# Attention and a gated feed-forward on one core: other blocks for the transposes of two attention units, and other places and engines for splitting the weights

## The chip, the cores and the metric

The kernel runs on one core of a Trainium2 chip. The metric is the time of one execution on the device in microseconds; the median of a few runs counts. TensorE (PE) multiplies, VectorE (DVE), ScalarE (ACT) and GpSimd (POOL) work on tiles in SBUF, SyncE (SP) starts the transfers. TensorE's results lie in PSUM, in banks that ScalarE or VectorE must empty before TensorE may write there again.

## The reference

Attention with a window (half of the heads plain, half dilated) over 8 batches, 8 heads, 576 positions, 64 dimensions; then a gated feed-forward with an RMS norm over all 4608 tokens.

```python
scores = scale * np.matmul(q, k.transpose(0, 1, 3, 2))
mask_plain = (rel >= 0) & (rel < window)                        # window 32
mask_dil = (rel >= 0) & (rel < window * dilation) & (rel % dilation == 0)
...
attn = np.exp(scores - np.max(scores, axis=-1, keepdims=True))
attn = attn / (np.sum(attn, axis=-1, keepdims=True) + 1e-09)
x = np.matmul(attn, v)            # to (4608, 512)
...
xn = x / np.sqrt(np.mean(x * x, axis=-1, keepdims=True) + 1e-06) * rms_g
g = xn @ w_gate                   # (512, 1536)
silu = g * (1.0 / (1.0 + np.exp(-g)))
return (silu * (xn @ w_val) @ w_out).astype(np.float32)
```

The weights arrive as 64-bit floats, and the kernel itself makes 32-bit ones of them.

## The kernel before

The tokens are cut into 16 units of 288 (`u`). A unit's attention comes in 14 bursts `(u, c, i)`: a pair of heads `c` and a block of queries `i`. A burst has three steps on TensorE, each in a place of its own: scores (`q`), transposing the probabilities (`t`), product with the values (`o`). Each unit's feed-forward has 12 turns `j`, each of three blocks (`part`): gate (`gate`, part 0), value (`val`, part 1), and the projection of the turn before (`proj`, part 2). Unit 1's attention is computed between the blocks of unit 0's feed-forward, unit 2's between those of unit 1's, and so on.

The order of instructions is written by the program itself: `now` counts the blocks, `later(dt, rank, fn)` puts work off by `dt` blocks, and `flush` issues what is due ahead of the block, by rank. `plan` writes into `events` in which block each burst's `q`, `t` and `o` stand. On every engine the instructions then run in this order, each as soon as its semaphores allow. `t` in the code below counts the blocks from the first gate of unit 0 (block 0 to 35 are unit 0's feed-forward, 36 to 71 unit 1's).

Up to unit 1 attention and feed-forward of unit 0 are computed in plain 32-bit floats. From then on each operand is split in a high part (`hi`, a cast) and the rest (`lo`, a subtraction), and three products are summed (`three`, lines 628 to 630). So the names that matter here are:

- `split_weight`: the cast of a weight into `hi` on ScalarE (L243) and, one block later, the subtraction into `lo` (L244), on VectorE or POOL. A weight pair shares one tile `lo`, which takes the place of the 32-bit pair before it. 36 weights are split, in the order of use, from block `SPLITS[0]` on; each must be there before unit 1 needs it (block 36 for the first).
- `decode`: VectorE makes a 32-bit pair out of the raw words in two instructions (L178 and L182), one in each block of unit 0; ScalarE (L160) and POOL (L163) prepare it.
- `split`: the high and low parts of a head's keys (L331 cast, L336 subtraction) and queries (L340, L345); its last step also starts the load of the head after next.
- `untranspose`: ScalarE copies a burst's transposes out of PSUM (L448); from unit 2 on VectorE subtracts that copy from them (L450).
- `bank`: gates and values share two banks. The bank of a value block `v` is that of the next turn's gate; the bank of a gate is that of the next turn's value. Transposes of part 0 and part 1 stand in spare columns of that block's bank, those of part 2 in the bank of the gate just used. Accesses of different engines to one bank are kept in order.
- `tanh` and `silu` (L667, L672) empty the gate's bank, `prod` (L685) the value's; `parts` makes `hhi` (L696) and `hlo` (L697) of it. `take` (L410) empties the bank `o`, `scores_max` (L362, L367) the bank `s`, `scores_norm` ends a burst's normalisation (L386, L387 and then L390 on ScalarE for unit 1 or L393 on POOL).

## Time and profile before

| | |
|---|---|
| median of 3 runs | 1143.98 us (1143.95 to 1144.72) |
| the profiled execution | 1143.79 us, span 1142.0 us |
| granted TensorE clock, mean | 0.997 |
| PE busy | 1119.9 us (98%) |
| DVE, ACT, POOL busy | 786.6 (69%), 714.2 (63%), 613.8 us (54%) |
| DMA | 82.19 MB, mean 72 GB/s |

The page has the busy time of each engine, the span in 40 slices, the chain of work that ended last and the costliest groups of instructions. Besides it the trace can be asked for the busy time in any stretch, for who waited for whom, for groups of instructions in a stretch, and for single instructions in order of time. An idle time in brackets stands with what ended it. Unit 0's feed-forward runs from about 40 to 127 us, unit 1's from 127.3 us on.

### The profile page before, as it was taken

Reading aid. Unit: us, or ns where it says so; the run is one execution under the profiler, and the core shown is the slowest. Engines: PE = TensorE matmul, PEld = TensorE weight load, DVE = VectorE, ACT = ScalarE, POOL = GpSimd, SP = SyncE. Lnnn points to the kernel's source line nnn. Section 1 sums busy time; section 2 is a strip of 40 time slices with the busy share of each in tenths; the row PEclk is TensorE's granted clock in tenths of the full one; section 3 lists DMA queues with packets and bytes.
Section 4 is the critical chain, followed back from the end, with each engine's and each line's share of the span. In section 5 each row is a group of like instructions: output and inputs, shape, how many; then the busy total and the mean of one; then the engine's idle time right before and its main releaser. Section 6 shows DMA issues by size and latency. Waiting matters only on the chain.

```text
span 1142.0 us, 25943 instructions
## 1 busy us (share of the span) xinstructions
PE 1119.9 (98%) x8371; PEld 1088.9 (95%) x8371; DVE 786.6 (69%) x2859; ACT 714.2 (63%) x2622; POOL 613.8 (54%) x1073
## 2 busy tenths in 40 slices
PE   8998989999999999999999999999999999999998
PEld 7776789999999999999999999999999999999998
DVE  7878874868768586776758677675867758586411
ACT  6795676756757576675757666575765757576311
POOL 8234576655656465565646555464655646465211
PEclk9999999999999999999999999999999999999999
DMA  9655210312212131221213112121211312120000
GB/s 253 184 208 204 77 51 26 104 41 71 64 36 84 38 95 43 75 67 31 81 40 97 46 50 84 38 82 41 75 60 47 95 33 79 42 79 15 5 19 21
DMA packets 61545, 82.19 MB, mean 72 GB/s; under 512 B 7298, under 2 KB 41090, under 8 KB 61410
## 3 DMA queue, kind: packets, MB, share of 16 engines
q1 hardware_dynamic: 61410, 80.54, 23.8%
q8 instruction: 67, 1.10, 0.4%
q14 instruction: 68, 0.56, 0.2%
HBM read 71.08 MB, written 9.44 MB: 71 GB/s over the span
## 4 chain that ended last, share of the span: by engine, by line
PE 86%; DVE 5%; ACT 4%; issue 2%; POOL 2%; POOLq 0%; DVEq 0%; ACTq 0%
PE v L628 9%; PE acc L628 8%; PE g L628 8%; PE acc L629 8%; PE v L629 8%; PE g L630 8%; PE v L630 8%; PE g L629 8%; PE acc L630 8%; PE s L495 3%; PE o L483 3%; PE o L484 1%; PE busy L745 1%; ACT t L377 1%; DVE raw L178 1%
## 5 line engine op out<-in xcount | busy, mean ns | idle before, releaser
L697 POOL TENSOR_TENSOR hlo<-th,hhi 128x288 fp32r<-128x288 f32 x180 | 145.4, 808 | 206.2 <-ACT hhi L696 153.8
L630 PE MATMUL acc<-hhi,lo 128*128 128x288 f32 x720 | 212.3, 295 | 0.0
L393 POOL TENSOR_SCALAR t<-t,sum 72x72 f32<-72x72 f32 (+3 forms) x414 | 153.4, 382 | 67.8 <-DVE sum L387 60.3
L630 PE MATMUL v<-xhi,lo 128*128 128x288 f32 x612 | 180.8, 295 | 0.0
L630 PE MATMUL g<-xhi,lo 128*128 128x288 f32 x612 | 180.6, 295 | 0.0
L377 ACT ACTIVATE t<-t,sum 96x128 f32<-96x128 f32 (+3 forms) x448 | 166.1, 375 | 9.7 <-DVE sum L367 9.1
L696 ACT CAST hhi<-th 128x288 fp32r<-128x288 f32 x180 | 78.1, 434 | 142.0 <-DVE th L685 140.2
L306 POOL TENSOR_TENSOR vlo<-vt,vhi 128x128 fp32r<-128x128 f32 x196 | 93.6, 478 | 107.2 <-ACT vhi L302 92.4
L667 ACT ACTIVATE th<-g 128x288 f32<-128x288 f32 x180 | 73.7, 410 | 106.8 <-PE g L630 85.5
L630 PEld LDWEIGHTS acc<-hhi,lo 128*128 128x128 f32 x720 | 135.6, 188 | 0.0
L423 DVE TENSOR_TENSOR xraw<-o,xraw 64x72 f32<-64x72 f32 (+1 forms) x364 | 99.2, 273 | 50.6 <-ACT xraw L413 44.5
L672 DVE SCALAR_TENSOR_TENSOR th<-th,g 128x288 f32<-128x288 f32 x180 | 80.3, 446 | 70.3 <-ACT th L667 70.3
L630 PEld LDWEIGHTS v<-xhi,lo 128*128 128x128 f32 x612 | 115.4, 189 | 0.0
L630 PEld LDWEIGHTS g<-xhi,lo 128*128 128x128 f32 x612 | 115.0, 188 | 0.0
L628 PE MATMUL g<-xhi,hi_g 128*128 128x288 f32 x357 | 110.7, 310 | 1.9 <-DVE pt L450 1.5
L628 PE MATMUL acc<-hhi,hi_o 128*128 128x288 f32 x360 | 110.9, 308 | 0.0
L336 POOL TENSOR_TENSOR ks<-qk,ks 128x288 fp32r<-128x288 f32 (+2 forms) x112 | 108.8, 986 | 0.0
L685 DVE TENSOR_TENSOR th<-th,v 128x288 f32<-128x288 f32 x180 | 81.5, 453 | 39.6 <-PE v L630 31.2
L629 PE MATMUL acc<-hlo,hi_o 128*128 128x288 f32 x360 | 107.0, 297 | 0.0
L362 DVE TENSOR_TENSOR t<-s,mask 96x256 f32<-96x256 f32 (+3 forms) x196 | 71.5, 365 | 49.7 <-PE s L495 44.4
L413 ACT COPY xraw<-o 64x72 f32<-64x72 f32 (+1 forms) x364 | 93.9, 258 | 11.8 <-PE o L484 9.7
L629 PE MATMUL g<-xlo,hi_g 128*128 128x288 f32 x322 | 94.8, 295 | 0.0
(189 smaller groups left out, 3588.9 us busy)
## 6 DMA issues: line engine op xcount, KB each, us to landing
qk<-in_qk_dram SPq DMA_DIRECT2D x60, 288.0 KB, 2.8
vt<-in_v_dram SPq DMA_DIRECT2D x196, 64.0 KB, 1.9
qk<-in_qk_dram SPq DMA_DIRECT2D x30, 352.0 KB, 3.0
out_dram<-ot SPq DMA_DIRECT2D x64, 144.0 KB, 1.9
qk<-in_qk_dram SPq DMA_DIRECT2D x30, 304.0 KB, 2.8
raw<-in_w_gate_dram SPq DMA_DIRECT2D x12, 512.0 KB, 4.8
raw<-in_w_val_dram SPq DMA_DIRECT2D x12, 512.0 KB, 4.5
raw<-in_w_out_dram SPq DMA_DIRECT2D x12, 512.0 KB, 4.2
```

What stands on the lines that cost most here:

```text
L306: G.tensor_tensor(out=vl, in0=vs.pop(b), in1=vh, op=ALU.subtract)
L336: ek.tensor_tensor(out=ks[:, 1, :nkt], in0=kr, in1=ks[:, 0, :nkt], op=ALU.subtract)
L377: A.activation(out=t[:nq, a, :n], in_=t[:nq, a, :n], func=AF.Exp, scale=-1.0, bias=sm[:nq, a, 0:1], accum_out=sm[:nq, a, 1:2] if u or i % ...
L393: (V if u == 0 and (c, i) > (NC - 1, 0) else G).tensor_scalar(out=t[:nq, a, :n], in0=t[:nq, a, :n], scalar1=sm[:nq, a, 3:4], scalar2=1.0, ...
L413: A.copy(out=to[a * D:(a + 1) * D], in_=o[a * D:(a + 1) * D, (2 + a) * nq:(3 + a) * nq])
L423: V.tensor_tensor(out=to[rows], in0=o[rows, a * nq:(a + 1) * nq], in1=to[rows], op=ALU.add)
L628: PE.matmul(out, wh[:, cc, :], xh, start=start, stop=False)
L629: PE.matmul(out, wh[:, cc, :], xl, start=False, stop=False)
L630: PE.matmul(out, wl[:, cc, :], xh, start=False, stop=stop)
L672: V.scalar_tensor_tensor(out=t, in0=t, scalar=1.0, in1=g, op0=ALU.add, op1=ALU.mult)
L685: V.tensor_tensor(out=t, in0=t, in1=v_ps[:, :U], op=ALU.mult)
L697: G.tensor_tensor(out=lo, in0=t, in1=hi, op=ALU.subtract)
```

## The change

Five edits. First, the table of blocks for unit 1's bursts and a new one like it for unit 2's: `q` in parts 0 and 1, so `t` (five blocks on) in parts 2 and 0, where before unit 1's stood mostly in 0 and 1, and unit 2's, spread evenly over more blocks, in all three. Unit 2's first scores stand in block 33 in place of 30. When a unit's sum and norm stand is unchanged. Second, splitting of weights in unit 0: in blocks of part 2 from 5 to 30, nine of them, where before it was every even block from 4 to 30, fourteen. Third, from block 35 on (before: 37) one weight in each block: in odd blocks VectorE now does the cast as well as the subtraction, in even blocks ScalarE the cast and POOL the subtraction, as before. Fourth, unit 2's first two heads are split six blocks later, with the keys' subtraction on VectorE instead of POOL. Fifth, all sums of unit 1's squares are on VectorE (two of three were on POOL).

```diff
-SPLITS = 4, 31, 37
+SPLITS = 5, 31, 35
-EARLY, LAST = (-6, -9), 17
+SCORES = {1: (-3, -2, 0, 1, 3, 4, 6, 7, 9, 10, 12, 13, 15, 16),
+          2: (-3, -2, 0, 1, 3, 4, 6, 7, 9, 10, 12, 13, 15, 16)}
+EARLY, LAST = -9, 17
...
-    def split_weight(kind, j, e):
+    def split_weight(kind, j, e, alone):
...
-        A.copy(out=hi, in_=single(kind, j))
+        (e.tensor_copy if alone and e is V else A.copy)(out=hi, in_=single(kind, j))
         later(1, 5.5, lambda: e.tensor_tensor(out=lo, in0=single(kind, j), in1=hi, op=ALU.subtract))
...
-            later(1, 0.4, lambda: (V if c == NC - 1 else G).tensor_tensor(out=xsq[u], in0=xsq[u], in1=sq, op=ALU.add))
+            later(1, 0.4, lambda: (V if c == NC - 1 or u == 1 else G).tensor_tensor(out=xsq[u], in0=xsq[u], in1=sq, op=ALU.add))
...
-                        later(5 + a, 9, lambda a=a: split(NNAT, a, (1, 2, 2, 3), G, V))
+                        later(11 + a, 9, lambda a=a: split(NNAT, a, (1, 2, 2, 3), V, V))
...
-        events.setdefault(base + o_at[-1] + (4 if u == 1 else 3), {})["sum"] = u
-        events.setdefault(base + o_at[-1] + (4, 7, 5)[min(u, 2)], {})["apply"] = u
+        last = base + (o_at[-1] if u < NNAT else LAST + 8)
+        events.setdefault(last + (4 if u == 1 else 3), {})["sum"] = u
+        events.setdefault(last + (4, 7, 5)[min(u, 2)], {})["apply"] = u
...
-        q_at = [LAST - (LAST - EARLY[u > NNAT]) * (nb - 1 - k) // (nb - 1) for k in range(nb)]
+        q_at = [LAST - (LAST - EARLY) * (nb - 1 - k) // (nb - 1) for k in range(nb)]
         t_at, o_at = [t + 5 for t in q_at], [t + 8 for t in q_at]
-        if u < NNAT:
-            q_at = (-4, -2, -1, 1, 2, 4, 6, 7, 8, 10, 11, 13, 14, 16)
-            t_at, o_at = [t + 5 for t in q_at], [t + 7 for t in q_at]
+        if u <= NNAT:
+            q_at = SCORES[u]
+            t_at, o_at = [t + 5 for t in q_at], [t + (7 if u < NNAT else 8) for t in q_at]
...
-                if used and (t >= SPLITS[2] or t % 2 == 0 and SPLITS[0] <= t < SPLITS[1]):
-                    later(0, 6, lambda: split_weight(*used.pop(0), V if t < SPLITS[1] or t % 2 else G))
+                if used and (t >= SPLITS[2] or part == 2 and SPLITS[0] <= t < SPLITS[1]):
+                    later(0, 6, lambda: split_weight(*used.pop(0), V if t < SPLITS[1] or t % 2 else G, t >= SPLITS[2]))
```

What it moves, at three places. In the rows the name before the arrow is what is written; names carry unit, turn or burst and a running number, `x2` is twice in a row. The changed kernel's line numbers are higher by four. First, TensorE in unit 0, from the end of the value block of turn 1 to the gate block of turn 2; before:

```order
L625 MATMUL v_0_1_696<-xn_3_623,f_1_332 128x288
L465 MATMUL v_0_1_696<-ident_64,t_1_0_2_598 128x96 x2
L492 MATMUL s_1_1_2_701<-qk_1_1_118 96x128 x2
L625 MATMUL acc_0_0_718<-h_0_640,f_2_529 128x288
L625 MATMUL acc_0_1_720<-h_0_640,f_2_529 128x288
L625 MATMUL acc_0_2_722<-h_0_640,f_2_529 128x288
L625 MATMUL acc_0_3_724<-h_0_640,f_2_529 128x288
L474 MATMUL o_1_0_1_726<-pt_1_0_1_678,v_1_0_150 128x192
L625 MATMUL g_0_2_742<-xn_0_616,f_2_529 128x288
```

and after:

```order
L629 MATMUL v_0_1_686<-xn_3_620,f_1_332 128x288
L478 MATMUL o_1_0_0_692<-pt_1_0_0_652,v_1_0_150 128x192
L496 MATMUL s_1_1_2_691<-qk_1_1_118 96x128 x2
L629 MATMUL acc_0_0_711<-h_0_631,f_2_529 128x288
L629 MATMUL acc_0_1_713<-h_0_631,f_2_529 128x288
L629 MATMUL acc_0_2_715<-h_0_631,f_2_529 128x288
L629 MATMUL acc_0_3_717<-h_0_631,f_2_529 128x288
L469 MATMUL t_0_1_719<-ident_64,t_1_0_2_622 128x96 x2
L478 MATMUL o_1_0_1_720<-pt_1_0_1_673,v_1_0_150 128x192
L629 MATMUL g_0_2_740<-xn_0_613,f_2_529 128x288
```

The transposes have left the value's bank `v_0_1` and stand behind the projection, in a tile of their own. Second, VectorE in unit 0 around the end of turn 8's value block; before:

```order
L178 SCALAR_TENSOR_TENSOR raw_13_1044<-raw_13_1044 128x1024
L345 TENSOR_TENSOR qs_2_0_1146<-qk_2_0_1026,qs_2_0_1146 64x288
L182 SCALAR_TENSOR_TENSOR f_13_1133<-f_13_1133,raw_13_1044 128x1024
L672 SCALAR_TENSOR_TENSOR h_8_1181<-h_8_1181,g_0_8_1176 128x288
L345 TENSOR_TENSOR qs_2_1_1162<-qk_2_1_1028,qs_2_1_1162 64x288
L244 TENSOR_TENSOR lo_5_1169<-f_5_739,hi8_g3_1092 128x512
L178 SCALAR_TENSOR_TENSOR raw_14_1089<-raw_14_1089 128x1024
L685 TENSOR_TENSOR h_8_1181<-h_8_1181,v_0_8_1191 128x288
```

and after:

```order
L182 SCALAR_TENSOR_TENSOR raw_13_1040<-raw_13_1040 128x1024
L186 SCALAR_TENSOR_TENSOR f_13_1121<-f_13_1121,raw_13_1040 128x1024
L248 TENSOR_TENSOR lo_3_1134<-f_3_599,hi4_o0_1014 128x512
L676 SCALAR_TENSOR_TENSOR h_8_1162<-h_8_1162,g_0_8_1157 128x288
L182 SCALAR_TENSOR_TENSOR raw_14_1081<-raw_14_1081 128x1024
L689 TENSOR_TENSOR h_8_1162<-h_8_1162,v_0_8_1168 128x288
```

The two subtractions of unit 2's queries have moved behind the tenth value block, and the weight's stands ahead of the gate's L672 (L676 after), once in a turn. Third, VectorE in unit 1, with what each instruction waits for where it waits; before, in turn 5:

```order
L450 TENSOR_TENSOR pt_2_2_3_1982<-g_1_5_1957,pt_2_2_3_1982 72x2x72 [waits Activation_49]
L672 SCALAR_TENSOR_TENSOR th_1_5_1980<-th_1_5_1980,g_1_5_1957 128x288 [waits Pool_49]
L345 TENSOR_TENSOR qs_3_1_1950<-qk_3_1_1726,qs_3_1_1950 64x288 [waits DMAHW2_49]
L244 TENSOR_TENSOR lo_14_1955<-f_14_1171,hi28_o8_1954 128x512 [waits Pool_49]
L685 TENSOR_TENSOR th_1_5_1980<-th_1_5_1980,v_1_5_1999 128x288 [waits DVE_49,PE_49]
```

and after, in turn 3:

```order
L247 CAST hi19_o5_1706<-f_9_943 128x512
L390 TENSOR_REDUCE sum4_90<-sum4_90 72x2
L391 RECIPROCAL sum4_90<-sum4_90 72x2 [waits DVE_49]
L454 TENSOR_TENSOR pt_2_1_2_1736<-g_1_3_1708,pt_2_1_2_1736 128x192 [waits Activation_49]
L366 TENSOR_TENSOR t_2_2_2_1742<-s_2_2_2_1721,mask_77 72x2x72 [waits PE_49,Pool_49]
L371 ISA t_2_2_2_1742,sum1_87<-s_2_2_2_1721,t_2_2_2_1742 72x72 [waits DVE_49]
L371 ISA sum1_87 72x1
L371 ISA t_2_2_2_1742,sum1_87<-s_2_2_2_1721,t_2_2_2_1742 72x72
L371 ISA sum1_87 72x1
L676 SCALAR_TENSOR_TENSOR th_1_3_1734<-th_1_3_1734,g_1_3_1708 128x288 [waits Pool_49]
L349 TENSOR_TENSOR qs_2_7_1698<-qk_2_7_1538,qs_2_7_1698 64x288 [waits DMAHW5_49]
L248 TENSOR_TENSOR lo_9_1667<-f_9_943,hi19_o5_1706 128x512
```

The cast (L247) now stands on VectorE too, a block ahead of the subtraction of the same weight. The weights of a pair have changed sides: VectorE takes the second one, and its subtraction no longer waits for POOL; of the ten that did in unit 1, three near the end (of pairs 14, 16 and 17) still do.

## The prediction

> **What bounds the kernel now.** I read the page's first rows, then the busy time by stage, then what TensorE (PE) waited for, then the single waits. Busy time by stage (columns: stretch, its length, busy us of PE, weight load, VectorE (DVE), ScalarE (ACT), GpSimd (POOL) with counts, granted clock, DMA share, GB/s):
>
> ```profile
> span 1142.0 us, 25943 instructions
> ...
> 45.00:127.30 82.30, 74.56 (x352) 58.13 (x350) 72.10 (x154) 58.80 (x172) 30.76 (x29) 0.98 0.52 182
> 127.30:184.50 57.20, 50.01 (x368) 48.18 (x368) 38.94 (x136) 42.72 (x151) 40.59 (x62) 0.97 0.22 63
> 200.00:1100.00 900.00, 899.78 (x7011) 896.33 (x7010) 626.69 (x2382) 567.41 (x2145) 498.01 (x897) 1.00 0.20 59
> ```
>
> From 200 to 1100 us PE is idle for 900 - 899.78 = 0.2 us. Nothing the change does can shorten or relieve that. The time to be had lies in two stages: the feed-forward of unit 0 (45 to 127.3 us, PE idle 82.30 - 74.56 = 7.74) and that of unit 1 up to its tenth gate block (127.3 to 184.5, idle 57.20 - 50.01 = 7.19). Both are where the change works. What ended PE's waits in them (total, times, longest):
>
> ```profile
> PE v L628 <- DVE pt L450: 4.4, 3, 1.9
> PE g L625 <- DVE h L685: 3.1, 1, 3.1
> PE g L625 <- ACT pt L448: 2.4, 2, 1.6
> PE g L628 <- DVE pt L450: 1.5, 1, 1.5
> PE acc L625 <- DVE sum L386: 1.0, 1, 1.0
> PE o L474 <- ACT xraw L410: 0.9, 1, 0.9
> PE o L479 <- ACT xraw L410: 0.7, 1, 0.7
> PE g L628 <- DVE th L685: 0.6, 1, 0.6
> PE g L628 <- issue: 0.3, 1, 0.3
> ```
>
> Every wait but the last 0.3 is for a PSUM bank that VectorE or ScalarE had not emptied, or for a weight. They sum to 14.9. Two of them are followed by a lower granted clock (same columns as the first table):
>
> ```profile
> 105.00:110.00 5.00, 5.00 (x19) 3.79 (x18) 3.85 (x7) 1.77 (x3) 0.73 (x1) 0.66 0.24 88
> 110.00:115.00 5.00, 5.00 (x24) 3.92 (x23) 4.49 (x6) 1.66 (x6) 1.99 (x4) 1.00 0.58 210
> ...
> 165.00:170.00 5.00, 4.06 (x21) 4.06 (x22) 4.58 (x14) 3.80 (x14) 4.02 (x6) 0.69 0.21 51
> 175.00:180.00 5.00, 5.00 (x42) 4.96 (x41) 1.86 (x7) 4.55 (x16) 3.99 (x7) 1.00 0.09 26
> ```
>
> At 0.66 PE did 19 matmuls where the next row has 24: 5/24 x 5 = 1.0 us lost. At 0.69 it did 21 in 4.06 busy us, where 42 in 5 would give 34: 13/8.4 = 1.5 us. So at most 14.9 + 2.5 = 17.4 us can be won.
>
> **Unit 0: what goes and what comes.** The longest wait, in single rows (start, us, engine, line, tiles, idle time before):
>
> ```profile
> 104.70 0.51 PE L625 MATMUL g<-xn,f 128*128 128x288 f32 x1 [3.08 <-DVE h L685]
> ...
> 95.77 2.98 POOL L336 TENSOR_TENSOR ks<-qk,ks 128x288 fp32r<-128x288 f32 x2
> ...
> 98.12 0.94 DVE L345 TENSOR_TENSOR qs<-qk,qs 64x288 fp32r<-64x288 f32 x1
> 99.10 2.04 DVE L182 SCALAR_TENSOR_TENSOR f<-f,raw 128x1024 uint32<-128x1024 uint32 x1
> 101.06 0.44 DVE L672 SCALAR_TENSOR_TENSOR h<-h,g 128x288 f32<-128x288 f32 x1
> 101.53 0.89 DVE L345 TENSOR_TENSOR qs<-qk,qs 64x288 fp32r<-64x288 f32 x1
> 102.45 0.69 DVE L244 TENSOR_TENSOR lo<-f,hi_g 128x512 fp32r<-128x512 f32 x1
> 103.06 1.22 DVE L178 SCALAR_TENSOR_TENSOR raw<-raw 128x1024 uint32<-128x1024 uint32 x1
> 104.20 0.45 DVE L685 TENSOR_TENSOR h<-h,v 128x288 f32<-128x288 f32 x1
> 104.56 0.45 DVE L435 TENSOR_TENSOR sq<-sq,sq 128x288 f32<-128x288 f32 x1
> ```
>
> The gate block needs the bank of the value block before it, which L685 empties. Ahead of L685 stand two subtractions of unit 2's first heads (0.94 + 0.89) and a weight's (0.69), and L182 took 2.04 where its twin L178 takes 1.22. In the new order those three are gone from this place (the heads are split six steps later, fewer weights are split here): 0.94 + 0.89 + 0.69 + 0.82 = 3.34 > 3.08, so the wait goes and with it the 1.0 us of slow clock. The heads come back on VectorE behind the tenth value block, with their keys' two subtractions moved over from POOL. No row shows those on VectorE; L435, as wide, takes 0.45. There POOL no longer has the 2.98 us stretch that slowed VectorE.
>
> The 2.4 us (1.6 + 0.8) were gate blocks waiting for ScalarE's copy of transposes out of the value's bank, which itself waits for L685 on that bank. In the new order nothing is transposed there. The 0.8 goes. Of the 1.6 only the copy (0.3, the mean of L448 below) and one burst's reductions that move behind L685 (0.3, estimated from their place) come off, 0.6; the decoding ahead of L685 remains. The 0.9 (o for xraw) hung behind such a copy on ScalarE: gone. The 1.0 (acc) waited for the last weight's decoding, which two score bursts delayed on VectorE; these move behind it, so it goes too.
>
> VectorE's load in this stage: 72.10, less 5 weight subtractions (5 x 0.69 = 3.4), less two of unit 2's bursts that move behind 127 us (0.8 each, from the rows of L362 and L367 below: 0.33 + 2 x 0.24; 1.6), plus two L435 taken from POOL (0.9) and two key subtractions (0.9), less the stretched time above (0.9 of L345 and 0.8 of L182, 1.7): 67 us of at least 76. It keeps up. On SP's queue the loads of unit 2's third head and later ones move with the split that issues them, the first of them behind the last weight's:
>
> ```profile
> qk<-in_qk_dram SPq DMA_DIRECT2D x60, 288.0 KB, 2.8
> ```
>
> They land in 2.8 us and are read four blocks later, some 9 us (82.3 us hold 36 - 1 blocks): hidden, and 2.8 less than 9 leaves cover if one is late. The work of units 3 to 15 keeps its order, and so do the sum and the spread of unit 2's root; they cost nothing.
>
> What is new: transposes and the output of a burst both stand behind the projection, so a late normalisation now stops PE there. No row prices it: nothing if ScalarE is on time, 2.3 if it cost what the two largest ScalarE waits did (1.6 + 0.7). I take 1.0, nearer the first, as ScalarE drops five of its weight casts here. Unit 0: 3.1 + 1.0 + 0.8 + 0.6 + 0.9 + 1.0 - 1.0 = **6.4 us won**.
>
> **Unit 1.** Groups of the stage 127 to 187 us (busy us, mean ns of one | idle before, releaser), a page row for a cast-like instruction, and three single rows:
>
> ```profile
> L345 DVE TENSOR_TENSOR qs<-qk,qs 64x288 fp32r<-64x288 f32 x6 | 5.8, 974 | 0.2
> L367 DVE CUSTOM_DVE_ANT_0 t<-s,t 72x72 f32<-72x72 f32 (+2 forms) x24 | 5.0, 243 | 0.4
> L244 DVE TENSOR_TENSOR lo<-f,hi_v 128x512 fp32r<-128x512 f32 x3 | 4.7, 1572 | 2.6 <-POOL lo L244 2.6
> L362 DVE TENSOR_TENSOR t<-s,mask 72x144 f32<-72x144 f32 (+2 forms) x12 | 3.9, 329 | 0.5 <-PE s L495 0.5
> L244 DVE TENSOR_TENSOR lo<-f,hi_g 128x512 fp32r<-128x512 f32 x4 | 2.8, 692 | 3.0 <-POOL lo L244 2.9
> ...
> L243 ACT CAST hi_o<-f 128x512 fp32r<-128x512 f32 x8 | 4.9, 618 | 0.0
> L448 ACT CAST pt<-v 72x144 fp32r<-72x144 f32 (+1 forms) x5 | 1.5, 292 | 7.9 <-DVE th L685 7.8
> ...
> L244 POOL TENSOR_TENSOR lo<-f,hi_g 128x512 fp32r<-128x512 f32 x4 | 5.1, 1286 | 0.0
> ...
> L166 DVE TENSOR_SCALAR f<-f 128x1024 uint32<-128x1024 uint32 x2 | 1.4, 686 | 0.0
> ...
> 162.01 3.34 DVE L244 TENSOR_TENSOR lo<-f,hi_v 128x512 fp32r<-128x512 f32 x1
> ...
> 182.70 0.69 DVE L244 TENSOR_TENSOR lo<-f,hi_g 128x512 fp32r<-128x512 f32 x1 [1.78 <-POOL lo L244]
> 183.31 0.45 DVE L685 TENSOR_TENSOR th<-th,v 128x288 f32<-128x288 f32 x1
> ```
>
> Three things to see. VectorE idles before L244 for POOL's half of the weight pair before (2.6 + 2.9 in two groups). At 182.70 this holds L685 up by 1.78, and that is PE's wait of 1.5. In the new order the pairs start one step over: POOL takes the first of a pair, VectorE the second, and ten of VectorE's subtractions that waited for POOL become three, all near the end. Second, ScalarE stands 7.8 us behind L685 with value transposes in its hand; no such copies are left. Third, L345 has a mean of 974 where L435 took 0.45 for as many columns, and L244 once took 3.34 where its group beside it has 692: with POOL busy, VectorE's operations on two SBUF operands are stretched.
>
> Removed: 1.5 (the POOL wait); 0.7 (o behind a value copy on ScalarE); and 0.5 for ScalarE's lighter queue, which no row prices: between nothing and the 2.5 that the waits for pt hold beside the longest (4.4 - 1.9), nearer nothing since VectorE has a part in each. The other 4.5 and the slow clock (1.5) hang on stretched VectorE operations and I leave them. Added on VectorE: 14 casts, for which no row stands. Bounds: half of L166, which has one SBUF operand and twice the width, 0.34; the whole subtraction L244, 0.69. I take 0.34, the same kind of operand: 14 x 0.34 = 4.8 (9.7 at the upper bound). Then 3 more subtractions, 2.1, and the two bursts, 1.6. VectorE: 38.94 + 8.5 = 47.4 of 57.2. POOL has two more subtractions, 2.6: 43.2. ScalarE loses 9 casts, 9 x 0.618 = 5.6. So VectorE goes from 68% to 83%, close enough that a stretched operation finds no idle time behind it: I set 1.0 of new waiting (0 where all hide; 8.5 less the 5.5 of POOL waits freed = 3.0 where none does). Unit 1: 1.5 + 0.7 + 0.5 - 1.0 = **1.7 us won**.
>
> The Trainium skill, "VectorE: DVE Perf Modes", section "Mode 2×_2P — use both read ports for one tensor", has a copy of one fp32 SBUF tensor run at two elements a cycle; at its 0.96 GHz that gives an estimate of 512/2/0.96 = 267 ns, 3.7 us for the 14 in place of 4.8. No run here shows a cast on VectorE yet.
>
> **Sum.** 6.4 + 1.7 = 8.1. The profiled execution took 1143.79 (span 1142.0 and 1.8 around it), 0.2 under the median of the runs, 1143.98. 1143.79 - 8.1 = 1135.7; against the median **1135.9 us**.
>
> **Rivals.**
> B: VectorE becomes the bound in unit 1. Casts cost 0.69: 9.7 + 2.1 + 1.6 - 5.5 = 7.9 more on VectorE, of which half lands on the banks' handoffs, 4.0, that is 3.0 beyond the sum: 1138.9, and 1140.4 with another slow-clock stretch of 1.5. For it: 83% load in an in-order queue. Against: ScalarE and POOL waits of VectorE end.
> C, slower: GpSimd and VectorE starve each other. 17 operations more on VectorE's SBUF side fall in a stage where POOL rises from 71% to 76%. A starved one costs 3.34 - 0.69 = 2.65. If 5 of them are, 13 us come on VectorE; where its idle time of 9.8 (57.2 - 47.4) lies elsewhere PE stands 13 us longer, against 9.1 won (8.1 + 1.0): 1143.98 + 13 - 9.1 = 1147.9. It decides from four starved at a bank's handoff. Against: only one of the seven in the groups shown was starved that long, though POOL was 71% busy.
> The Trainium skill's "GPSIMD Engine Reference", section "Key points", says that GpSimd shares its SBUF interfaces with VectorE and contends with instructions on two SBUF inputs or in a two-port mode. By that rule the new casts can be hit as well as the subtractions; the trace agrees for the subtractions alone.
> D, no change: unit 0 is paced by decoding weights rather than by the waits, so that they only move. VectorE was busy 72.1 of 82.3 us there. Then only unit 1's 1.7 is left: 1142.3. Against: the sum above gives it 10 us of room.
>
> **Chances.** Forecast 0.57 (its own range 1130.0, with the 2.0 of new waits at zero and 3.8 of the 4.5 gone as well, to 1138.5). B 0.22, D 0.11, C 0.10. A change below 0.2% (2.3 us) cannot be told from none here. Faster: forecast and B, 0.79; same: D, 0.11; slower: C, 0.10. The range reaches from 1130.0 over B and D to 1142.4.
>
> **What would show it.** In the changed profile: no wait near 3 us of PE for h L685 in unit 0, clock 1.00 throughout 100 to 110; no group of L448 with source v in units 0 and 1; VectorE's L244 idle for POOL under 1 us in all; casts on VectorE near 0.34; PE idle in the two stages about 2.3 and 5.5. The prediction is wrong if PE's waits for L450 or L685 in unit 1 grow past 6 us, if a cast's mean exceeds 0.7, or if unit 0 ends later than 123 us.

## The result and the profile after

The changed kernel takes 1137.8 us (median of four runs, 1137.03 to 1138.89) against 1144.35 us of the kernel before beside it (1143.95 to 1145.27): 6.55 us less, a ratio of 0.9934, 95% interval 0.9918 to 0.9950. The forecast was 1135.9, 8.1 us less. Run again later on another occasion it took 1137.88 us, a ratio of 0.9928 (0.9911 to 0.9944). The profiled execution took 1138.89 us, its span is 4.9 us shorter than that of before. Line numbers of the changed kernel are higher by four: L628 is L632, L448 and L450 are L452 and L454, L243 and L244 are L247 and L248, L345 is L349, L367 is L371, L685 is L689.

The busy time by stage of the changed kernel (columns as in the prediction). It is cut at the same three places of TensorE's work in both kernels: the last two matmuls of unit 0's first gate block, the first gate block of unit 1, and the block of unit 1 that started at 184.51 us before.

```profile
36.60:119.45 82.85, 80.13 (x395) 63.72 (x394) 74.26 (x175) 61.91 (x183) 28.63 (x24) 1.00 0.55 189
119.45:179.75 60.30, 53.35 (x378) 50.19 (x376) 49.91 (x155) 39.44 (x148) 43.27 (x66) 0.94 0.22 64
179.75:1137.10 957.35, 952.55 (x7411) 948.48 (x7411) 646.64 (x2426) 584.10 (x2191) 515.59 (x919) 1.00 0.19 56
```

And the same cuts of the kernel before:

```profile
36.10:127.29 91.19, 83.13 (x395) 64.82 (x394) 80.58 (x180) 64.19 (x191) 31.73 (x30) 0.98 0.51 174
127.29:184.51 57.22, 50.02 (x369) 48.20 (x369) 38.95 (x136) 42.74 (x151) 40.59 (x62) 0.97 0.22 63
184.51:1142.00 957.49, 953.58 (x7414) 949.67 (x7414) 642.36 (x2422) 583.48 (x2192) 513.38 (x919) 1.00 0.19 56
```

Unit 0 is 91.19 - 82.85 = 8.3 us shorter, unit 1 is 60.30 - 57.22 = 3.1 us longer, the rest is the same within 0.2, and the opening ahead of the first cut is 0.5 longer. Unit 0's 8.3 are 5.3 of idle time (8.06 before, 2.72 after) and 3.0 of busy time. Of the 3.0, 1.7 or more is the slow clock (0.98 against 1.00): at 0.66 the five microseconds from 105 on lose 0.34 x 5 = 1.7, and splits_alone below, with the old table but a clock of 1.00 in this stage, has 80.73 us busy there, 2.4 less than before. The rest is work that went elsewhere. Unit 1's stage has nine matmul records more (378 against 369), seven of them those of one burst of unit 2 (two scores, two transposes, three products with values); unit 0 has as many as before (395), since four scores of unit 1 came into it from the opening. Its idle time hardly moved: 7.20 before, 6.95 after. In the second profile of the changed kernel the two stages are 82.7 and 59.1 us, so the 3.1 is a high value and 1.9 a low one; the difference is slow clock (0.94 against 0.97 in this stage).

What ended PE's waits in the changed kernel, from 40 to 195 us (total, times, longest):

```profile
PE s L499 <- DVE sum L371: 3.7, 5, 1.1
PE v L632 <- DVE pt L454: 2.6, 3, 1.3
PE v L629 <- ACT pt L452: 1.8, 1, 1.8
PE s L499 <- DVE qs L349: 0.6, 1, 0.6
PE o L483 <- ACT xraw L414: 0.5, 1, 0.5
```

The waits for `h`, for `acc` and most of those for `pt` are gone. A kind of wait that the kernel before did not have leads the list: scores that wait for the bank `s`, which VectorE's reductions (L366, L371) empty. Groups on VectorE from 119 to 182 us (busy us, mean ns of one | idle before), where the casts (L247) are seen for the first time:

```profile
L248 DVE TENSOR_TENSOR lo<-f,hi_g 128x512 fp32r<-128x512 f32 x5 | 6.4, 1288 | 0.1
L248 DVE TENSOR_TENSOR lo<-f,hi_o 128x512 fp32r<-128x512 f32 x4 | 5.7, 1413 | 0.0
L247 DVE CAST hi_o<-f 128x512 fp32r<-128x512 f32 x4 | 5.1, 1264 | 0.0
L247 DVE CAST hi_v<-f 128x512 fp32r<-128x512 f32 x4 | 4.2, 1038 | 0.1
...
L248 DVE TENSOR_TENSOR lo<-f,hi_v 128x512 fp32r<-128x512 f32 x4 | 2.8, 692 | 0.1
L247 DVE CAST hi_g<-f 128x512 fp32r<-128x512 f32 x5 | 2.1, 418 | 0.0
```

A cast takes 0.42 us where it is undisturbed (the last row), and (5.1 + 4.2 + 2.1) / 13 = 0.88 in the mean. A subtraction takes 0.69 undisturbed and (6.4 + 5.7 + 2.8) / 13 = 1.15 in the mean. VectorE's waits for GpSimd's subtraction are gone, 0.1 us of idle time is left.

### The profile page after: what moved, and what is told of

It is laid out like the page before. It is cut to its first block, busy times and chain, and to the rows that moved or that the text cites. A ratio compares the mean times of both kernels' runs of the same rounds, so it can differ in the third digit from the quotient of the medians.

```text
span 1137.1 us, 25931 instructions
## 1 busy us (share of the span) xinstructions
PE 1119.5 (98%) x8371; PEld 1088.7 (96%) x8371; DVE 795.5 (70%) x2875; ACT 708.7 (62%) x2608; POOL 615.7 (54%) x1071
## 4 chain that ended last, share of the span: by engine, by line
PE 91%; DVE 5%; ACT 1%; issue 1%; DMA 1%; POOL 1%; POOLq 0%; SPq 0%; ACTq 0%
PE acc L632 9%; PE v L632 8%; PE g L632 8%; PE acc L633 8%; PE acc L634 8%; PE v L633 8%; PE g L633 8%; PE v L634 8%; PE g L634 8%; PE s L499 3%; PE o L487 3%; PE acc L629 2%; PE v L629 1%; PE o L488 1%; PE busy L749 1%; PE g L629 1%
## 5 line engine op out<-in xcount | busy, mean ns | idle before, releaser
L397 POOL TENSOR_SCALAR t<-t,sum 72x72 f32<-72x72 f32 (+3 forms) x414 | 153.1, 382 | 69.7 <-DVE sum L391 61.1
L381 ACT ACTIVATE t<-t,sum 96x128 f32<-96x128 f32 (+3 forms) x448 | 166.1, 375 | 11.4 <-DVE sum L371 10.9
L676 DVE SCALAR_TENSOR_TENSOR th<-th,g 128x288 f32<-128x288 f32 x180 | 80.4, 447 | 68.3 <-ACT th L671 68.3
L632 PE MATMUL g<-xhi,hi_g 128*128 128x288 f32 x357 | 111.0, 311 | 0.1
L632 PE MATMUL acc<-hhi,hi_o 128*128 128x288 f32 x360 | 111.0, 308 | 0.0
L366 DVE TENSOR_TENSOR t<-s,mask 96x256 f32<-96x256 f32 (+3 forms) x196 | 71.5, 365 | 53.5 <-PE s L499 42.6
L689 DVE TENSOR_TENSOR th<-th,v 128x288 f32<-128x288 f32 x180 | 81.4, 452 | 38.0 <-PE v L634 30.1
L340 POOL TENSOR_TENSOR ks<-qk,ks 128x288 fp32r<-128x288 f32 (+2 forms) x110 | 104.5, 964 | 0.3 <-ACT ks L335 0.3
```

The costliest lines, as they stand in the source:

```text
L340: ek.tensor_tensor(out=ks[:, 1, :nkt], in0=kr, in1=ks[:, 0, :nkt], op=ALU.subtract)
L381: A.activation(out=t[:nq, a, :n], in_=t[:nq, a, :n], func=AF.Exp, scale=-1.0, bias=sm[:nq, a, 0:1], accum_out=sm[:nq, a, 1:2] if u or i % ...
L397: (V if u == 0 and (c, i) > (NC - 1, 0) else G).tensor_scalar(out=t[:nq, a, :n], in0=t[:nq, a, :n], scalar1=sm[:nq, a, 3:4], scalar2=1.0, ...
L632: PE.matmul(out, wh[:, cc, :], xh, start=start, stop=False)
L676: V.scalar_tensor_tensor(out=t, in0=t, scalar=1.0, in1=g, op0=ALU.add, op1=ALU.mult)
L689: V.tensor_tensor(out=t, in0=t, in1=v_ps[:, :U], op=ALU.mult)
```

## The experiments

Ratios are to the kernel before on the same chip, with 95% intervals. The stages are those cut above, from one profile of each kernel. The runs were made on four occasions, on which the kernel before itself took 1144.35 us (changed), 1145.35 (casts_scalar, lows_vector, splits_old, heads_old), 1145.29 (tables_alone, scores_first, lows_vector_first, lows_vector_half) and 1146.3 (the others), so microseconds of different occasions compare only roughly.

| kernel | us | ratio | unit 0 (PE idle) | unit 1 (PE idle) |
|---|---|---|---|---|
| changed | 1137.8 | 0.9934 (0.9918 to 0.9950) | 82.85 (2.7) | 60.3 (6.95) |
| changed, again | 1137.88 | 0.9928 (0.9911 to 0.9944) | 82.7 (2.6) | 59.1 (6.9) |
| tables_alone | 1139.79 | 0.9954 (0.9940 to 0.9969) | 86.1 (5.3) | 58.5 (7.3) |
| splits_alone | 1142.37 | 0.9963 (0.9949 to 0.9978) | 85.7 (5.0) | 59.0 (7.6) |
| splits_old (tables and heads) | 1141.22 | 0.9964 (0.9951 to 0.9976) | 86.2 (5.4) | 58.2 (7.0) |
| heads_old (tables and splits) | 1139.44 | 0.9947 (0.9931 to 0.9963) | 85.5 (3.8) | 59.3 (7.35) |
| casts_scalar | 1137.03 | 0.9921 (0.9905 to 0.9937) | 82.8 (2.7) | 58.2 (6.3) |
| lows_vector | 1137.58 | 0.9929 (0.9914 to 0.9944) | 82.7 (2.6) | 58.9 (8.3) |
| scores_first | 1138.18 | 0.9937 (0.9923 to 0.9950) | 82.6 (2.6) | 59.1 (8.4) |
| lows_vector_first | 1134.47 | 0.9905 (0.9890 to 0.9920) | 82.8 (2.6) | 56.1 (5.4) |
| lows_vector_half | 1135.22 | 0.9909 (0.9891 to 0.9927) | 82.8 (2.6) | 56.6 (5.8) |
| first_opening | 1134.85 | 0.9901 (0.9885 to 0.9917) | 83.1 (2.8) | 56.1 (5.4) |
| thirds_opening | 1133.24 | 0.9888 (0.9871 to 0.9905) | 83.5 (3.0) | 54.4 (4.0) |

**Which part won unit 0.** Four kernels have one or two of three parts of the change: the tables (the first edit), the splitting of weights (the second and third) and unit 2's heads (the fourth). The repeat of the whole change, run beside the last ones:

> The changed kernel once more, for a comparison on the same chip as the three runs beside it: 0.9934 of before, within 0.0015.

It came out as expected. The tables alone:

```diff
 (before)
-EARLY, LAST = (-6, -9), 17
+SCORES = {1: ..., 2: ...}
+EARLY, LAST = -9, 17
...
+            q_at = SCORES[u]
...
```

> The kernel before with the new score tables of units 1 and 2 alone (and the sum and the spread of unit 2's root where the changed kernel has them); the splitting of weights and of unit 2's first heads as before. The forecast's steps for the tables: the waits for ScalarE's copies of value transposes go (0.8 and a part of 1.6 in unit 0, 0.9 for o), and in unit 1 o's 0.7; the long wait for h (3.1) and its slow clock stay. So unit 0 is 2 to 3 us shorter. In unit 1, theory T (the new spacing of scores, in seven of thirteen pairs one step apart, makes the scores wait for the s bank) says one burst's work more and new waits for s of 2 to 3 us, but L448's and L450's waits fall by as much: 58 us in place of 57.2. In all 1142 to 1143. If the tables were the whole cause of the gain it would be 1138.

It was 1139.79, more won than the forecast's steps gave. In unit 0 the 0.8 for `pt` and the wait for `xraw` went as forecast, and the one for `acc` too; the 1.6 in the opening stayed (1.8). The wait for `h` came in two pieces (3.4 us in all, the longest 2.6), but the clock was at 1.00, where the forecast kept the slow clock. In unit 1 it did what theory T said: 58.5 us with waits for `s` (2.4). The splitting alone:

```diff
 (before)
-SPLITS = 4, 31, 37
+SPLITS = 5, 31, 35
...
-        A.copy(out=hi, in_=single(kind, j))
+        (e.tensor_copy if alone and e is V else A.copy)(out=hi, in_=single(kind, j))
...
-                if used and (t >= SPLITS[2] or t % 2 == 0 and SPLITS[0] <= t < SPLITS[1]):
+                if used and (t >= SPLITS[2] or part == 2 and SPLITS[0] <= t < SPLITS[1]):
...
```

> The kernel before with the splitting of weights alone changed (9 weights in unit 0, 27 in unit 1, every other one whole by VectorE); score tables and unit 2's heads as before. By the forecast's steps: unit 0 loses 0.7 of the 3.1 (the weight's subtraction) and the 1.0 of the last weight's decoding; in unit 1 1.5 (VectorE's wait for GpSimd's subtraction) goes and 1.0 comes: 1142 to 1142.7. Theory S: in unit 1 the casts, stretched beside GpSimd, cost more than the freed wait, 1 to 2 us lost there: 1143.5 to 1145. That the parts only pay together (the bank's handoff in unit 0 is held by heads and weights alike) would give no change, within 1.

1142.37 is inside the forecast's microseconds, but beside it the kernel before took 1146.3 (1143.97 to 1150.29), and the ratio, 0.9963, is more than the 0.998 to 0.999 that the forecast stands for. The wait for `h` shrank from 3.08 to 2.35, by the 0.7 that the forecast had for the weight's subtraction. But unit 1 was not shortened: 59.0, with one wait of 1.7 us for the bank `s`, though the old table is in place. The two kernels with one of these parts taken out of the change:

```diff
 (changed; splits old)
-SPLITS = 5, 31, 35
+SPLITS = 4, 31, 37
...
-        (e.tensor_copy if alone and e is V else A.copy)(out=hi, in_=single(kind, j))
+        A.copy(out=hi, in_=single(kind, j))
...
-                if used and (t >= SPLITS[2] or part == 2 and SPLITS[0] <= t < SPLITS[1]):
+                if used and (t >= SPLITS[2] or t % 2 == 0 and SPLITS[0] <= t < SPLITS[1]):
...
```

> The changed kernel with the splitting of weights undone: 14 in unit 0 and 22 in unit 1 as before, casts on ScalarE, pairs begun by VectorE with GpSimd behind; the score tables and the place of unit 2's first heads stay new. Forecast's steps: unit 0 keeps the gain of the heads and loses only the part of the five subtractions and casts (0.7 of the 3.1, and the 1.0 of the last weight): unit 0 ends 1 to 1.7 us later than in the changed kernel; unit 1 gets its wait of VectorE for GpSimd's subtractions back (1.5) by the forecast, but loses the casts. Theory S: unit 1 back to 57.2 or below, in all 1135.5 to 1136.5. Theory T: unit 1 stays at 60 and the waits for the s bank remain: 1138.8 to 1140.

```diff
 (changed; heads old)
-                        later(11 + a, 9, lambda a=a: split(NNAT, a, (1, 2, 2, 3), V, V))
+                        later(5 + a, 9, lambda a=a: split(NNAT, a, (1, 2, 2, 3), G, V))
```

> The changed kernel with unit 2's first two heads split where they were before (from the fifth step behind the last burst of unit 1's third part, their keys' subtractions on GpSimd). The forecast's step: the wait of the gate block of unit 0 for h (3.1) and the slow clock behind it (1.0) come back in part, since the weight's subtraction (0.69) that stood there too is gone: 2.4 to 4.1 us slower than the changed kernel, 1140.2 to 1141.9. Rival: the wait was due to the number of weights split there, and two heads more find room in VectorE's idle time: 1137.8, within 0.7.

Both lose. splits_old came out above every number expected of it (1135.5 to 1136.5, 1138.8 to 1140): unit 0 lost 3.4 us, where 1 to 1.7 was expected. heads_old lies between its forecast (1140.2 to 1141.9) and its rival (1137.8, within 0.7), and its interval overlaps that of the changed kernel; what shows its loss is the stage, 85.5 against 82.8. PE's waits in unit 0, first with the splits old, then with the heads old:

```profile
PE g L628 <- DVE h L688: 2.7, 2, 2.5
PE v L628 <- ACT pt L451: 1.8, 1, 1.8
```

```profile
PE g L629 <- DVE h L689: 1.9, 1, 1.9
PE v L629 <- ACT pt L452: 1.8, 1, 1.8
```

With the heads at the old place the wait stands where it stood, 1.9 us; with the splits old it moves with the heads to the turn two further on, 2.5 us, where a weight's subtraction and a head's again stand ahead of `h` (single rows of VectorE, splits old):

```profile
112.53 1.00 DVE L348 TENSOR_TENSOR qs<-qk,qs 64x288 fp32r<-64x288 f32 x1
113.56 1.17 DVE L247 TENSOR_TENSOR lo<-f,hi_v 128x512 fp32r<-128x512 f32 x1
114.65 0.44 DVE L688 TENSOR_TENSOR h<-h,v 128x288 f32<-128x288 f32 x1
```

Only with both moved is it gone. So the parts do not add up. Of PE's idle time in unit 0 (8.06 before) the tables alone win 2.7 us, the splits alone 3.1, both 4.3 and the whole change 5.3; the heads, worth nothing on top of the tables alone (5.4 against 5.3), are worth 1.1 on top of both (3.8 to 2.7). The lengths of the stage (5.1, 5.5, 5.7 and 8.3 us less) hold the slow clock besides, which followed the wait for `h` in the kernel before (3.08 us) and in heads_old (1.89), and did not in tables_alone (2.59), splits_alone (2.35) and splits_old (2.50). The fifth edit, the sums of squares on VectorE, is in splits_old and heads_old and not in the other two; no run has it alone.

**Why unit 1 lost.** Its idle time hardly shrank, though the waits that the forecast counted did. Two theories: the casts and subtractions on VectorE are starved by GpSimd (S), or the new table makes the scores wait (T). First the casts back on ScalarE:

```diff
 (changed)
-        (e.tensor_copy if alone and e is V else A.copy)(out=hi, in_=single(kind, j))
+        A.copy(out=hi, in_=single(kind, j))
```

> The changed kernel with one thing undone: the 14 weights that VectorE took whole in unit 1's feed-forward get their cast (hi) from ScalarE again, VectorE keeps the subtraction. Theory S (starvation): unit 1 lost about 3 us in the changed kernel because VectorE's casts and subtractions on SBUF are stretched beside GpSimd's, and the 13 casts there cost 11.0 us in place of 4.8. Without them VectorE has 11 us more room and unit 1 goes back from 60.3 us to about 57.5: 1135.0. Theory T (table): the loss comes from the new score table, whose scores now wait for the s bank; the casts matter little: 1137.8, within 1. Theory Q (queue): the casts are worth having because ScalarE's queue is what the banks wait for, and giving 13 x 0.62 = 8.0 us back to it makes copies late: 1139.5 or more.

The time is the same as the changed kernel's within the intervals, as theory T had it, and the waits for `s` stay (3.2 us). VectorE fell from 49.91 to 41.95 us busy and nothing much came of it: the casts' place is not the cause, and not a gain either. Next the subtractions:

```diff
 (changed, casts on ScalarE as above)
-                    later(0, 6, lambda: split_weight(*used.pop(0), V if t < SPLITS[1] or t % 2 else G, t >= SPLITS[2]))
+                    later(0, 6, lambda: split_weight(*used.pop(0), V, t >= SPLITS[2]))
```

> As casts_scalar, and every weight's subtraction in unit 1 is done by VectorE, so GpSimd loses 13 subtractions of some 1.4 us there (18 us of 43). VectorE's own busy time by unstretched prices: 49.9 - 11.0 (casts) + 13 x 0.69 (9.0) = 48. Theory S: VectorE's operations on SBUF shrink towards 0.69 once GpSimd runs less beside them, waits of L454 and L371 fall to a third: unit 1 under 57 us, 1134. Theory T: 1137.8, within 1, with the same waits for the s bank. A third way: 27 subtractions in one queue are too many for VectorE, each step has one of 0.69 ahead of the bank's copies: 1140 or more.

Theory S was right on the price and wrong on the time. The 27 subtractions took 20.4 us (0.76 each; 8.0 + 6.5 + 5.9 in three groups), and no value block waited for `pt` any more. But the time stood still, since the waits for `s` rose to 5.8. One of them, first ScalarE, then VectorE and PE:

```profile
128.22 0.62 ACT L247 CAST hi_v<-f 128x512 fp32r<-128x512 f32 x1
128.74 0.41 ACT L671 ACTIVATE th<-g 128x288 f32<-128x288 f32 x1
129.04 0.30 ACT L452 CAST pt<-g 128x192 fp32r<-128x192 f32 x1
```

```profile
129.38 0.36 DVE L454 TENSOR_TENSOR pt<-g,pt 128x192 fp32r<-128x192 f32 x1 [0.47 <-ACT pt L452]
129.65 0.41 DVE L366 TENSOR_TENSOR t<-s,mask 96x256 f32<-96x256 f32 x1
130.10 0.29 DVE L371 CUSTOM_DVE_ANT_0 t<-s,t 96x128 f32<-96x128 f32 x1
...
130.75 0.45 PE L499 MATMUL s<-ks,qs 128*96 128x256 f32 x2 [1.48 <-DVE sum L371]
```

The reductions that free the bank `s` stand behind L454, which waits for ScalarE's copy, which stands behind a tanh and a weight's cast. VectorE is not overloaded here: it is blocked at the head of its queue, for 0.47 us. That is a third theory, W. In the changed kernel itself only one of the four waits for the bank is of this kind, the 0.84 at 153.82: VectorE stood idle there for 1.33 before L454. Ahead of the other three (1.06, 0.48 and 0.70) VectorE works without idle time, behind casts and subtractions that were stretched. The last of them, VectorE first, then PE:

```profile
161.01 1.41 DVE L247 CAST hi_v<-f 128x512 fp32r<-128x512 f32 x1
...
162.60 0.28 DVE L454 TENSOR_TENSOR pt<-g,pt 72x144 fp32r<-72x144 f32 x1
```

```profile
163.67 0.48 PE L499 MATMUL s<-ks,qs 128*72 128x144 f32 x2 [0.70 <-DVE sum L371]
```

Theory W is tried by the order alone:

```diff
 (changed)
-            later(1, 0.7, lambda: scores_max(*q, s_ps))
+            later(1, 0.15 if q[0] == NNAT else 0.7, lambda: scores_max(*q, s_ps))
```

> The changed kernel with one rank changed: for unit 2's bursts VectorE reduces the scores (L366, L371) ahead of the lower part of the transposes (L454) that comes in the same step, in place of behind it. Theory W: the new waits for the s bank in unit 1 (3.7 us) come because L454 stands ahead of the reductions and itself waits for ScalarE's copy; then the waits for s fall below 1.5 and unit 1 gets about 2 us shorter: 1135.5 to 1136. Rival: they come because VectorE is late altogether (casts and subtractions stretched), so that the wait only moves from s to pt: 1137.8, within 1.

No gain, so W alone is not it either. Waits for `pt` fell (1.4) and those for `s` rose to 4.2 in unit 1, of which 3.2 is one wait. Here it is, VectorE first, then GpSimd in the same time, then PE:

```profile
157.82 4.17 DVE L349 TENSOR_TENSOR qs<-qk,qs 64x288 fp32r<-64x288 f32 x1
...
162.63 0.30 DVE L366 TENSOR_TENSOR t<-s,mask 72x144 f32<-72x144 f32 x1
```

```profile
156.83 0.79 POOL L701 TENSOR_TENSOR hlo<-th,hhi 128x288 fp32r<-128x288 f32 x1
157.58 0.86 POOL L340 TENSOR_TENSOR ks<-qk,ks 128x320 fp32r<-128x320 f32 x1
158.40 0.80 POOL L439 TENSOR_TENSOR sq<-sq,sq 128x288 f32<-128x288 f32 x1
159.16 0.88 POOL L340 TENSOR_TENSOR ks<-qk,ks 128x320 fp32r<-128x320 f32 x1
160.00 0.45 POOL L310 TENSOR_TENSOR vlo<-vt,vhi 128x128 fp32r<-128x128 f32 x1
160.41 1.26 POOL L248 TENSOR_TENSOR lo<-f,hi_v 128x512 fp32r<-128x512 f32 x1
```

```profile
163.50 0.33 PE L499 MATMUL s<-ks,qs 128*72 128x144 f32 x2 [3.19 <-DVE sum L371]
```

A subtraction of 0.46 us takes 4.17: it starts while GpSimd works off six subtractions and sums without a gap, and ends 0.3 us after the last of them (160.41 + 1.26 = 161.67 against 161.99). The last of the six is the weight's. Now both theories at once, the order and no weights on GpSimd; first with all casts on ScalarE (as in lows_vector), then with VectorE's casts kept, which the diff shows:

```diff
 (changed)
-            later(1, 0.7, lambda: scores_max(*q, s_ps))
+            later(1, 0.15 if q[0] == NNAT else 0.7, lambda: scores_max(*q, s_ps))
...
-                    later(0, 6, lambda: split_weight(*used.pop(0), V if t < SPLITS[1] or t % 2 else G, t >= SPLITS[2]))
+                    later(0, 6, lambda: split_weight(*used.pop(0), V, t >= SPLITS[2] and t % 2))
```

> lows_vector (all casts of unit 1 by ScalarE, all subtractions by VectorE) with the reductions ahead of L454 as in scores_first. In lows_vector each wait for s (5.8 us) had VectorE idle for 0.5 to 1.3 us on ScalarE's copy pt ahead of the reductions. Theory W: these idle times leave the path: s waits below 2, unit 1 from 58.9 to about 55.5, 1134. Rival: the copies being late is what counts, and the value blocks wait for pt in their place: 1137.5, within 1.

> The changed kernel with VectorE's casts kept on every other weight, every subtraction of unit 1 on VectorE, and the reductions ahead of L454. GpSimd has 13 subtractions less. Theory S says that the casts, which cost 0.85 in the mean beside GpSimd's subtractions, fall to the 0.42 of those that ran alone, and the subtractions from 1.2 to 0.76: VectorE 14 x 0.42 + 27 x 0.76 = 26.4, against 11.4 + 14.9 = 26.3 in the changed kernel, so no busier with 13 subtractions more, and ScalarE is lighter by 8 us than in lows_vector_first: 1133 to 1134.5. Rival: casts and subtractions in one queue are too many in one step, 1137.5 or more.

1134.47 and 1135.22: unit 1 at 56.1 and 56.6 us. The first is near its forecast (1134), the second 0.7 above the range it was given, with waits for `s` of 2.4 us where the first has 1.1. The second differs from scores_first in one thing only, the engine of 13 subtractions, and was 3.0 us faster though VectorE got them on top. Its groups from 117 to 182 us:

```profile
L248 DVE TENSOR_TENSOR lo<-f,hi_g 128x512 fp32r<-128x512 f32 x11 | 8.9, 805 | 0.1
L248 DVE TENSOR_TENSOR lo<-f,hi_v 128x512 fp32r<-128x512 f32 x8 | 5.9, 736 | 0.1
L248 DVE TENSOR_TENSOR lo<-f,hi_o 128x512 fp32r<-128x512 f32 x8 | 5.8, 724 | 0.1
...
L247 DVE CAST hi_g<-f 128x512 fp32r<-128x512 f32 x6 | 2.8, 461 | 0.0
L247 DVE CAST hi_o<-f 128x512 fp32r<-128x512 f32 x4 | 2.2, 550 | 0.0
L247 DVE CAST hi_v<-f 128x512 fp32r<-128x512 f32 x4 | 1.9, 486 | 0.0
```

14 casts take 6.9 us (0.49 each, 0.88 in the changed kernel) and 27 subtractions 20.6 (0.76, against 1.15): 27.5 us for 41 operations. In scores_first 14 casts took 10.9 and 13 subtractions 12.3 in the same stretch, 23.2 us for 27. So fourteen operations more cost VectorE 4.3 us, 0.31 each, less than half of the 0.69 that one takes undisturbed; and the queries' subtractions (L349) fell from 7.9 to 4.9 us, so that its busy time in unit 1 went down, from 50.38 to 48.78. Meanwhile 13 subtractions of some 1.4 us each left GpSimd. The gain needs both: the order without taking GpSimd's weights away (scores_first), or taking them away without the order (lows_vector, with all casts on ScalarE), left the time as it was.

**A version that beats both.** What is left in lows_vector_first is put down to ScalarE. Two attempts, both with the new order in the opening; the last two lines of the diff are in the second alone, which has VectorE do a third of the casts:

```diff
 (lows_vector_first)
-        later(1, 0 if u + j else 0.65, tanh)
-        later(1, 0.8, silu)
+        later(1, 0 if u + j else 2.5, tanh)
+        later(1, 0.8 if u + j else 2.6, silu)
...
-                    later(0, 6, lambda: split_weight(*used.pop(0), V, t >= SPLITS[2]))
+                    later(0, 6, lambda: split_weight(*used.pop(0), V, t >= SPLITS[2] and t % 3 == 2))
```

> lows_vector_first, and in unit 0's opening the first gate block's tanh behind the softmax of the bursts on ScalarE (rank 2.5 in place of 0.65, its product behind it). There the first value block in a bank waits 1.75 us for ScalarE's copy pt, which stands behind the tanh that waited 2.98 us for VectorE. If that order is the cause, the softmax fills that idle time and the wait falls by about 0.9: 1133.6. Rival: VectorE's product with the root, put behind the reductions by the same rank, makes the tanh later by as much: 1134.5, within 0.7.

> As first_opening, with VectorE doing the cast of every third weight too, the one that comes in the step of the projection (9 casts of 27). In lows_vector_first most of what is left in unit 1 (3.1 us put down to o, and 0.8 to 1.1 us of VectorE's idle time ahead of L454 each time) hangs on ScalarE's copy pt in the step behind a projection, where a cast of 0.61 stands ahead of it. Theory S with W: nine casts at 0.5 fit into VectorE's idle time there and the copy comes 0.6 us earlier: unit 1 from 56.1 to 54.5, 1132.3. Rival: VectorE is late by as much as ScalarE is earlier, as in lows_vector_half, where the waits for s came back: 1134 to 1135.

The opening brought nothing: the wait fell from 1.75 to 1.40 and 0.6 came back behind it as a wait for `h`; that rival was right. The third of the casts brought unit 1 to 54.4 us as theory S with W had it (54.5), with 4.0 us idle; the time lies between that theory's 1132.3 and its rival's 1134, and its runs overlap a little with those of first_opening (1133.45 to 1135.66). In all 1133.24 us (1132.55 to 1133.76) beside 1137.88 (1136.51 to 1139.39) of the changed kernel on the same chip, 4.6 us less, and 0.9888 of the kernel before. What is left in unit 1 is waits for `s` (2.1), `pt` (0.9), `o` (0.6) and `qs` (0.3).

## Why the prediction was right, and where it was not

**Unit 0: 6.4 forecast.** By idle time and clock it was 5.3 + 1.7 = 7.0. Term by term: the 3.1 for `h` went, and splits_old and heads_old show that it took both things that the sum counted, the heads' two subtractions and the weight's. The slow clock went; it was mis-sized at 1.0, for its 0.66 over 5 us loses 1.7. The 0.8, the 0.9 and the 1.0 (acc) went. The 0.6 did not: the wait for ScalarE's copy in the opening was 1.57 before and is 1.75 now, two blocks earlier. The -1.0 for new waits was 0.7 (one wait for `s`, just ahead of unit 1). The stage itself became shorter by 8.3, since a burst of unit 2 left it besides; the prediction took that burst off VectorE's load and did not say that PE's time for it appears in unit 1. This changes no sum, but 'unit 0 ends at' is then no test of the terms.

**Unit 1: 1.7 forecast, 0.3 of idle time won (7.20 to 6.95, and 6.9 in the second profile; the prediction had 5.5).** The 1.5 came: VectorE's wait for GpSimd's subtraction is gone, and with it more of the waits for `pt` than forecast, 4.4 + 1.5 before and 2.6 now. Of the 0.7 (o for xraw) 0.5 is still there. The term that was mis-sized is the new waiting: -1.0, and by the bounds at most 3.0; it was 3.7 for `s` (3.1 for the bank and 0.6 for the heads of the score). The prediction looked for it as load on VectorE, and the load came as it said: 49.91 of 60.30 us, 83%. What made the waits is three things. The table puts scores in neighbouring blocks seven times, where unit 2's even spread did it three times, so that the bank `s` must be emptied within one block, and tables_alone has these waits without any cast on VectorE (2.4 us). The reductions stand behind casts and subtractions that are stretched: so in three of the four waits of the changed kernel, and in the 1.7 us of splits_alone, which has the old table. And they stand behind an operation that waits for ScalarE: so in the fourth, and in lows_vector. The slow clock, which the prediction left at 1.5, is as it was in the second profile (0.97) and twice as long in the first (0.94).

**The cast, 0.34.** It is 0.42 undisturbed, over the 0.34 and over the estimate of 267 ns; in the mean it is 0.88, over the upper bound of 0.69 and over the 0.7 that the prediction named as a sign that it is wrong. This changed little: moving the casts away (casts_scalar) shifted the time by less than the intervals.

**The rivals.** B (VectorE the bound) has a number, 1138.9, that is nearer to the measured 1137.8 than the forecast's 1135.9, and it had the place right, the banks' handoffs. But VectorE's load as such was not what held them: casts_scalar has 8 us less of it and is no faster, and lows_vector_half has a larger share (48.78 of 56.6 us, against 49.91 of 60.3) and is faster. C named the mechanism that was there, starved operations: in unit 1 six casts and subtractions of the changed kernel took more than 1.3 us (L248 3.67, 2.50 and 1.63, L247 3.57, 1.41 and 1.40). Four of them stand ahead of a wait of PE's, the number from which C decides, but these waits are 1.34, 0.57, 0.70 and 0.65 us, 3.3 together, where C had 13. D (unit 0 paced by decoding) is refuted by unit 0's idle time.

**The sum.** 7.0 in unit 0 and 0.3 in unit 1, less nothing (second profile) or 1.7 (first) of slow clock there: 7.3 or 5.6, measured 6.55 between the medians. It was forecast 8.1. What failed is unit 1's term; that the total came as near as it did is in part luck, since the slow clock of unit 0 was worth 0.7 more than the sum had it.

## What to carry to other kernels

A table of places for work is to be read for each bank it uses: how many blocks lie between two uses, and what stands ahead, in the emptying engine's queue, of the operation that frees it; an operation there that waits for a third engine blocks it without any load. A weight's subtraction moved from GpSimd to VectorE cost VectorE little here (its busy time in the stage even fell, from 50.38 to 48.78 us), since its other operations on SBUF were held less. When two waits lie one behind the other, removing either alone shows no gain, and parts of a change tried singly then look worthless or look like the whole.

## What the hardware showed that was not expected

An operation of VectorE on two SBUF operands can be passed over by several of GpSimd's instructions in a row: L349 took 4.17 us for 0.46 until a row of six of them was over. It need not be the whole row: in splits_alone a subtraction of a weight (L244) took 3.35 us and ended at 162.79, while GpSimd's row went on to 165.18; the instruction of GpSimd beside its end (L306) took 0.87 in place of 0.46. And GpSimd's instructions with one tensor operand (L397) did not hold it: in scores_first L248 took 0.68 us from 155.69 on, beside two of them. The Trainium skill, "SBUF — State Buffer", section "SBUF: two separate sides", has the shared port pair held by one of the two engines for a whole instruction; the trace agrees for GpSimd's instructions on two tensors, and adds that the next one of GpSimd can have it again ahead of VectorE's that waits. Casts, with a single SBUF operand, are hit as well (1.26 us in the mean for hi_o beside 0.42), which fits that section's other case, an operation that uses two ports.

The clock is halved for a stretch, and it did not follow the length of the idle time. In rows of one microsecond the kernel before has 0.73, 0.50, 0.50 and 0.56 from 105 to 109 us, which loses 1.7 us of full speed; one of them:

```profile
107.00:108.00 1.00, 1.00 (x4) 0.62 (x3) 0.89 (x1) 0.00 (x0) 0.00 (x0) 0.50 0.00 0
```

The stretch from 166 us on in the kernel before and the one in the changed kernel's second profile lose 1.7 as well, that in its first profile 3.4 (0.77, six rows of 0.50, 0.82 from 161 to 169). In scores_first PE stood still for 3.19 us and the next rows kept 1.00; in the changed kernel it stood for 1.34 and got 0.65 and 0.66 in the next two rows of five. First scores_first, then the changed kernel (columns as in the stages):

```profile
160.00:165.00 5.00, 1.81 (x15) 1.61 (x14) 4.84 (x13) 1.14 (x4) 2.71 (x6) 1.00 0.26 75
165.00:170.00 5.00, 5.00 (x40) 4.82 (x39) 2.96 (x15) 4.12 (x17) 4.31 (x7) 1.00 0.26 75
```

```profile
160.54 0.40 PE L632 MATMUL v<-xhi,hi_v 128*128 128x288 f32 x1 [1.34 <-DVE pt L454]
```

```profile
160.00:165.00 5.00, 3.76 (x18) 3.44 (x19) 4.81 (x15) 1.68 (x6) 3.16 (x5) 0.65 0.24 75
165.00:170.00 5.00, 5.00 (x30) 4.92 (x30) 2.86 (x14) 2.99 (x14) 2.71 (x5) 0.66 0.26 75
```

What decides it stays open; no run was made for it.
